# A longer estimate for sending rows out on GpSimd, and a mask of taken tokens read from PSUM

## The chip, the cores and the metric

One Trainium2 chip; the kernel runs on 1 of its cores. The metric is device microseconds of one execution, median of several runs. Engines: TensorE (PE, with PEld for its weight loads), VectorE (DVE), ScalarE (ACT), GpSimd (POOL) and SyncE (SP), each with its own instruction stream that runs in the written order; semaphores hold an instruction until what it needs is there.

## The reference

```python
def reference(**kwargs):
    attn_out = _attn_ref(**attn_kwargs)          # B 4, H 8, S 576, D 64
    x = np.ascontiguousarray(attn_out.transpose(0, 2, 1, 3)).reshape(B * S, H * D)
    x = _moe_ref(x=x, **moe_kwargs)              # g(x @ w_in) @ w_out, 2304 x 512, d_ff 2048
    return _moe2_ref(x=x, **moe2_kwargs)

def _moe2_ref(x, w_gate, w1, w2):
    N, D = x.shape                               # 2304, 512; E 8, F 1024
    cap = N // E                                 # 288
    logits = x @ w_gate
    order = np.argsort(-logits.flatten())
    assigned = -np.ones(N, dtype=np.int64)
    counts = np.zeros(E, dtype=np.int64)
    for idx in order:
        tok, e = (int(idx) // E, int(idx) % E)
        if assigned[tok] >= 0 or counts[e] >= cap:
            continue
        assigned[tok] = e
        counts[e] += 1
        if (assigned >= 0).all():
            break
    out = np.zeros((N, D), dtype=np.float32)
    for e in range(E):
        mask = assigned == e
        h = np.maximum(x[mask] @ w1[e], 0.0)
        out[mask] = h @ w2[e]
    return out.astype(np.float32)
```

Attention with a forgetting bias, a dense feed-forward layer, and a layer of eight experts in which every expert gets exactly 288 tokens, given out greedily by the largest logit.

## The kernel before

Class `Attention` (0 to about 325 us) and class `Ffn` (to about 725 us) compute the first two layers; the change leaves them alone. The last 340 us belong to class `Route`, which gives tokens to experts, and class `Experts`, which computes them.

**The router.** It works in eight phases; each fills one expert. A phase (`Route.phase`) searches the logit from which on the expert is full: five steps, each a compare of all tokens' best logits with up to 128 thresholds on VectorE (`cmp`, 128 x 18 x 128), 18 small matmuls on TensorE that count (`rp<-OH,cmp`, L1128), a readback on VectorE (`jk`), one more small matmul (`rp<-fl,ones`, L1156) and a few tiny VectorE instructions (`du`, `th`) that make the next thresholds. Then the tokens of the expert get their places (`s1`, zero for a token that isn't taken), a list of their rows is made (`row`, sent by SP as `idx`), the logits of the full expert are taken out, and the tokens that got a place are taken out of `alive`. Much of the router's state, `alive` among it, lies in one PSUM tile (`state`); `s1`, `nb`, `OH`, `cmp` and `wj` lie in SBUF. In before a token is dead if `nb = (s1 < cap + 0.5) * s1` is not zero: `nb` reads `s1` twice, and the next instruction multiplies `alive` with `nb == 0`.

**The experts.** For each expert the 288 rows are gathered on GpSimd's queue (`xg<-x2d,idx`, three indirect DMAs), transposed on TensorE (`pt`, L1422) and split into a high part on ScalarE (`xh`) and a low part on VectorE (`xl`). The weights come by SP in pieces of 128x512 (`raw`), eight buffers in all; ScalarE makes the high part `wh`, and while the router works GpSimd makes the low part `wl = raw - wh` (L1219 is the line of the helper that issues all of these; tiles tell them apart). First layer: 96 matmuls `ph` (L1441) of 288 columns, relu on ScalarE (`hh`), low part on VectorE (`hl`). Second layer: 96 matmuls `py` (L1493), copied out (`y`), turned back (`po`, `yo`), and sent out on GpSimd's queue in three indirect DMAs (`out_dram<-yo,idx`), each with a one-element memset of `spacer` ahead of it.

**What sets the order.** All instructions are written once, in Python, and each engine runs them in that order. `Experts` keeps a model clock for the core (`self.clock`) and one for each of VectorE, ScalarE and GpSimd (class `Queue`, L1187 on, which adds a duration for each issued instruction). `tick` moves the clock with each matmul; when the clock passes the time at which the router's next step should be ready, the step is written, and the low parts `hl`, `xl` and `wl`, gathers and weight loads are written when the model says that their inputs are there. `can_split` holds a weight piece back when GpSimd's model clock is 1500 ns ahead or a gather is due within 1300 ns. A changed duration in the model so moves instructions on all engines, without changing any of them.

Of the kernel before, what the change touches and what calls it, by code (L numbers as in the profile page):

```python
# [18 lines left out]
OP = mybir.AluOpType  # L19
AX = mybir.AxisListType  # L20
PSUM = bass.MemoryType.PSUM
DRAM = bass.MemoryType.DRAM
# [834 lines left out]
class Route:  # L857
# [22 lines left out]
    def t(self, shape, dt, name, bufs=1):  # L880
        if name not in self.STATE:
            return self.c.tile(shape, dt, name=name, bufs=bufs)
        n = math.prod(shape[1:]) * (2 if dt == BF16 else 4) // 4
        if name not in self.places:
            self.places[name] = [self.used + b * n for b in range(bufs)]
            self.used += bufs * n
            assert self.used <= 512
        at = self.places[name].pop(0)
        self.places[name].append(at)
        a = self.st[:, at:at + n]  # L890
        a = a if dt == F32 else a.bitcast(dt)
        return a if len(shape) == 2 else a.rearrange("p (a b) -> p a b", b=shape[2])
# [111 lines left out]
    def phase(self, k):  # L1004

        nc, J, E = self.nc, self.J, self.E
        v, t = self.v, self.t
        more = k < E - 1
        e1 = t([128, 1], F32, "e1")
        if more:  # L1010
            yield from self.search()

            n, pd = self.n, self.pd
            q = t([128, E], F32, "q8")
            v.scalar_tensor_tensor(q, pd[:, :E], n, self.rank, op0=OP.is_equal, op1=OP.mult)
            v.tensor_reduce(e1, q, axis=AX.X, op=OP.max)
        else:
            v.tensor_copy(e1, self.left)

        wj = t([128, J], F32, "wj")  # L1020
        v.tensor_scalar(wj, self.w2, e1, None, op0=OP.is_equal)
        AT = t([128, 2, J], F32, "AT")
        if more:
            v.scalar_tensor_tensor(AT[:, 0], self.mx, self.tau, wj, op0=OP.is_gt, op1=OP.mult)
            v.scalar_tensor_tensor(AT[:, 1], self.mx, self.tau, wj, op0=OP.is_equal, op1=OP.mult)
        else:
            v.tensor_copy(AT[:, 0], wj)
            v.tensor_scalar(AT[:, 1], wj, 0.0, None, op0=OP.mult)

        run = t([128, 2 * J], BF16, "run")  # L1030
        ATf = AT.rearrange("p a j -> p (a j)")
        v.tensor_tensor_scan(run, ATf, self.iotf[:, 0:2 * J], 0.0, op0=OP.add, op1=OP.bypass)
        self.mark()
        ei = t([128, 1], I32, "ei", bufs=8)
        v.tensor_scalar(ei, e1, -1.0, float(E), op0=OP.mult, op1=OP.add)

        self.out[k] = [ei, None, getattr(v, "t", 0)]
        yield 200


        pp = self.ps()
        nc.tensor.matmul(pp[:, 0:1], self.lower, run[:, J - 1:J], start=True, stop=True)
        nc.tensor.matmul(pp[:, 1:2], self.lower, run[:, 2 * J - 1:2 * J], start=True, stop=False)
        nc.tensor.matmul(pp[:, 1:2], self.higher, run[:, J - 1:J], start=False, stop=True)
        def close():

            if more:
                pe = t([128, E], F32, "pe")
                v.tensor_scalar(pe, self.rank, e1, -2 * self.BIG, op0=OP.is_equal, op1=OP.mult)
                v.tensor_tensor(self.L, self.L, self.bj(pe, E), op=OP.add)  # L1050
                yield from self.pause()
                yield from self.wishes()
                yield from self.pause()

        if k:
            yield from close()
        s1 = t([128, J], F32, "s1", bufs=2)
        sT = t([128, J], F32, "sT")
        v.scalar_tensor_tensor(s1, run[:, :J], pp[:, 0:1], AT[:, 0], op0=OP.add, op1=OP.mult)
        v.scalar_tensor_tensor(sT, run[:, J:], pp[:, 1:2], AT[:, 1], op0=OP.add, op1=OP.mult)  # L1060
        v.tensor_tensor(s1, s1, sT, op=OP.add)
        yield from self.pause()
        self.jobs += self.tokens(k, s1)
        if k in (0, 1, E - 2, E - 1):

            self.job()
            self.job()
            self.mark()
            yield 540
            self.job()  # L1070
            self.job()
        if not k:
            yield from close()
        if more:

            nb = t([128, J], F32, "nb")
            v.scalar_tensor_tensor(nb, s1, self.cap + 0.5, s1, op0=OP.is_lt, op1=OP.mult)
            v.scalar_tensor_tensor(self.alive, nb, 0.0, self.alive, op0=OP.is_equal, op1=OP.mult)
            v.tensor_tensor(self.OH, self.OH, self.bc(self.alive, E), op=OP.mult)
            if k < E - 2:  # L1080
                yield from self.pause()
                self.cmp = self.compare16(self.thr0)
            v.tensor_tensor(self.w2, self.w2, self.alive, op=OP.mult)
            v.tensor_tensor(self.left, self.left, e1, op=OP.subtract)
# [102 lines left out]
class Queue:  # L1187
# [9 lines left out]
    def __getattr__(self, name):  # L1197
        fn = getattr(self.eng, name)

        def issue(*a, **kw):  # L1200
            tiles = [x for x in (*a, *kw.values()) if hasattr(x, "tensor")]
            out, done = tiles[0], self.at.written
            n = max(math.prod(x.shape[1:]) for x in tiles)
            t = max(self.t, self.at.clock)
            for x in tiles[1:]:
                if x.space == PSUM and x.tensor.name != self.at.route.st.tensor.name:
                    t = max(t, self.at.clock + 190)
                elif (x.tensor.name, x.offset) in done:
                    eng, ns = done[x.tensor.name, x.offset]
                    t = max(t, ns + (130 if eng is self else 190))  # L1210
            fixed = self.fixed + (65 if any(math.prod(x.shape[1:]) == 1 for x in tiles[1:]) and n > 1 else 0)
            if name == "indirect_dma_start":
                self.t = t + self.fixed + 1000
            else:
                two = all(x.space != PSUM and (x.dtype in (I16, BF16) or name in ("tensor_scalar", "tensor_copy"))
                          for x in tiles)
                self.t = t + fixed + (self.fast if two else self.column) * n
            done[out.tensor.name, out.offset] = self, self.t
            return fn(*a, **kw)  # L1219

        return issue
# [438 lines left out]
```

## Time and profile before

| | |
|---|---|
| median of 3 runs | 1036.65 us (1034.18 to 1041.91) |
| profiled execution | 1032.85 us, span 1031.1 us |
| mean granted TensorE clock | 0.981 |
| TensorE busy | 964.3 us, 94% of the span |
| VectorE, ScalarE, GpSimd busy | 74%, 48%, 33% |

Times in rows are microseconds from the span's start, durations of single instructions in the tile view are nanoseconds. `[5.94 <-DVE cmp L1219]` behind a row means that the engine stood idle for 5.94 us before it, until that instruction was done. Rows of equal instructions that follow each other are merged (`x6`). The granted clock is a share of full speed; TensorE's two levels are 1.2 and 2.4 GHz. Matmuls overlap, so a row's duration is longer than the distance to the next row.

### The profile page before, as it was taken

The page shows a single profiled execution, that of the slowest core. Times are in us where ns is not written, and L with a number is a line of the kernel's source. Part 1 is how long each engine was busy: PE and PEld are TensorE (multiplying, and loading weights), DVE is VectorE, ACT ScalarE, POOL GpSimd, SP SyncE. Part 2 cuts the span into 40 slices and gives each one's busy share as a digit, 9 for nine tenths or more (in the row PEclk, how much of TensorE's full clock was granted, in tenths as well). Part 3 has the DMA queues.
Part 4 walks back from the last instruction along what each step waited for, and adds up shares of the span by engine and source line. Part 5 has one row for each costly group of instructions (what it writes and reads, how often), then busy time and mean ns, then how long its engine had stood idle before and what let it go on. Part 6 is the DMA issues. An engine that isn't in the chain of part 4 may idle for free.

```text
span 1031.1 us, 18509 instructions
## 1 busy us (share of the span) xinstructions
PE 964.3 (94%) x6479; PEld 854.7 (83%) x6479; DVE 768.1 (74%) x2109; ACT 490.2 (48%) x961; POOL 338.8 (33%) x391
## 2 busy tenths in 40 slices
PE   6899999999979999999999999999889978989995
PEld 5777777777767989899889898899789868979995
DVE  6688888878857669799999998875568777775410
ACT  5777777767745542332332323430345424546431
POOL 3144454534421000000000000330778858873211
PEclk9999999999989999999999999999999989999998
DMA  5768777776667140030121300102555436557300
GB/s 130 161 165 194 200 201 191 200 194 173 189 203 246 54 147 29 21 102 22 31 93 31 113 11 11 62 11 81 159 165 172 157 115 190 165 147 222 118 24 24
DMA packets 124347, 126.86 MB, mean 123 GB/s; under 512 B 74178, under 2 KB 90818, under 8 KB 124124
## 3 DMA queue, kind: packets, MB, share of 16 engines
q1 hardware_dynamic: 104604, 89.79, 30.7%
q0 software_dynamic: 18592, 34.75, 11.6%
q10 hardware_dynamic: 1056, 1.12, 0.4%
q8 instruction: 51, 0.84, 0.3%
q14 instruction: 44, 0.36, 0.1%
HBM read 93.55 MB, written 27.50 MB: 117 GB/s over the span
## 4 chain that ended last, share of the span: by engine, by line
PE 58%; DVE 24%; DMA 5%; issue 5%; ACT 5%; POOL 1%; SPq 1%; another core or an unknown queue 0%; POOLq 0%; ACTq 0%; DVEq 0%
PE py L1493 8%; PE ph L1441 8%; PE ph L620 8%; PE po L333 6%; PE pst L301 6%; DVE junk L682 6%; PE px L661 3%; PE px L663 3%; PE px L662 3%; ACT u L629 3%; PE ps L249 2%; PE ps L250 2%; DVE u L628 2%; DVE gl L642 2%; PE rp L1128 2%
## 5 line engine op out<-in xcount | busy, mean ns | idle before, releaser
L1219 POOL TENSOR_TENSOR wl<-raw,wh 128x512 fp32r<-128x512 f32 x98 | 129.2, 1345 | 57.7 <-DMA raw<-in_moe_w_dram 33.8
L629 ACT ACTIVATE u<-u,half 128x384 f32<-128x384 f32 x96 | 59.3, 617 | 173.8 <-DVE u L628 169.0
L620 PE MATMUL ph<-xh,ih 128*128 128x384 f32 x384 | 130.8, 341 | 3.6 <-ACT ih L584 3.6
L620 PE MATMUL ph<-xh,il 128*128 128x384 f32 x384 | 130.6, 340 | 0.2 <-DVE il L592 0.2
L620 PE MATMUL ph<-xl,ih 128*128 128x384 f32 x384 | 130.5, 340 | 0.0
L333 PE MATMUL po<-E,V 128*128 128x320 f32 (+4 forms) x448 | 113.9, 383 | 0.4 <-ACT E L305 0.4
L663 PE MATMUL px<-oh,gl 128*128 128x512 f32 x240 | 95.3, 397 | 3.7 <-DVE gl L642 3.7
L661 PE MATMUL px<-oh,gh 128*128 128x512 f32 x240 | 95.2, 397 | 1.9 <-ACT x L670 1.8
L662 PE MATMUL px<-ol,gh 128*128 128x512 f32 x240 | 94.5, 394 | 0.0
L333 PEld LDWEIGHTS po<-E,V 128*128 128x128 f32 (+1 forms) x448 | 75.9, 194 | 20.5 <-issue 7.8
L682 DVE SCALAR_TENSOR_TENSOR junk<-x,gb 128x512 f32<-128x512 f32 x120 | 84.9, 737 | 4.5 <-ACT x L670 4.5
L682 DVE SCALAR_TENSOR_TENSOR junk<-wt,gb 128x512 f32<-128x512 f32 x128 | 82.9, 685 | 0.0
L1493 PE MATMUL py<-hh,wh 128*128 128x288 f32 x256 | 81.0, 317 | 0.0
L1219 ACT ACTIVATE wh<-raw 128x512 fp32r<-128x512 f32 x128 | 75.9, 624 | 9.2 <-DMA raw<-in_moe_w_dram 8.0
L1441 PE MATMUL ph<-xh,wh 128*128 128x288 f32 x256 | 79.4, 310 | 0.4 <-ACT xh L1219 0.4
L1441 PE MATMUL ph<-xl,wh 128*128 128x288 f32 x256 | 79.0, 309 | 0.5 <-DVE xl L1219 0.4
L620 PEld LDWEIGHTS ph<-xh,ih 128*128 128x128 f32 x384 | 72.7, 189 | 8.0 <-ACT ih L584 3.9
L1441 PE MATMUL ph<-xh,wl 128*128 128x288 f32 x256 | 78.4, 306 | 0.0
L1493 PE MATMUL py<-hl,wh 128*128 128x288 f32 x256 | 77.5, 303 | 0.0
L1493 PE MATMUL py<-hh,wl 128*128 128x288 f32 x256 | 77.2, 302 | 0.0
L620 PEld LDWEIGHTS ph<-xl,ih 128*128 128x128 f32 x384 | 72.7, 189 | 3.4
L506 POOL TENSOR_TENSOR co<-cm,ce 128x512 f32<-128x512 f32 x32 | 40.5, 1264 | 104.2 <-ACT cm L505 99.4
(228 smaller groups left out, 2487.9 us busy)
## 6 DMA issues: line engine op xcount, KB each, us to landing
raw<-in_moe_w_dram SPq DMA_DIRECT2D x128, 256.0 KB
r<-in_moe_w_in_dram SPq DMA_DIRECT2D x16, 512.0 KB
r<-in_moe_w_out_dram SPq DMA_DIRECT2D x16, 512.0 KB
xg<-xd SPq DMA_DIRECT2D x6, 768.0 KB
x2d<-x SPq DMA_DIRECT2D x36, 128.0 KB
Y<-Y POOLq DMA_DIRECT2D x15, 288.0 KB
nk<-in_k_dram SPq DMA_DIRECT2D x32, 128.0 KB
nq<-in_q_dram SPq DMA_DIRECT2D x32, 128.0 KB
```

The costliest lines, as they stand in the source:

```text
L301: nc.tensor.matmul(pst[u][:, cols], l, r, start=first, stop=last, skip_group_check=u == "c" or u == "b")
L333: nc.tensor.matmul(t[:, 256 + c0:256 + g1], V[:b - a, kb, 64 * h:64 * h + 128], E[:b - a, e0:e0 + g1 - c0], start=i == 0, stop=i == len(or ...
L506: nc.gpsimd.tensor_tensor(out, f(m), f(e), op=OP.mult)
L620: nc.tensor.matmul(p[:, :G], a[:, s], b, start=n == 0, stop=n == 11)
L629: nc.scalar.activation(u, u, AF.Square, bias=self.half, scale=0.5)
L661: nc.tensor.matmul(px[t][:, cols], gh[:, s], oh[:, cols], start=i == 0, stop=False)
L662: nc.tensor.matmul(px[t][:, cols], gh[:, s], ol[:, cols], start=False, stop=False)
L663: nc.tensor.matmul(px[t][:, cols], gl[:, s], oh[:, cols], start=False, stop=last)
L682: self.nc.vector.scalar_tensor_tensor(junk, x(), 1.0, self.gb[:, e], op0=OP.mult, op1=OP.mult, accum_out=out[:, e:e + 1])
L1219: return fn(*a, **kw)
L1441: self.nc.tensor.matmul(p[:, :self.C], a[:, cols], b, start=c == 0 and i == 0, stop=c == 3 and i == 2)
L1493: nc.tensor.matmul(p[:, :C], a[:, o:o + 128], b[:, fb], start=fb == 0 and i == 0, stop=fb == 7 and i == 2)
```

## The change

Two edits. In the model of `Queue`, an indirect DMA whose target is in DRAM (a send-out) is charged 1300 ns instead of 1000; a gather keeps 1000. In `Route.phase`, the update of `alive` is written with three instructions in place of two: tokens not taken in this phase (`s1 < 0.5`) times `alive`, tokens beyond the capacity (`s1 > cap + 0.5`) times `alive`, and their sum. Every one of the three has one operand in PSUM.

```diff
@@ -1074,8 +1074,9 @@
         if more:
 
             nb = t([128, J], F32, "nb")
-            v.scalar_tensor_tensor(nb, s1, self.cap + 0.5, s1, op0=OP.is_lt, op1=OP.mult)
-            v.scalar_tensor_tensor(self.alive, nb, 0.0, self.alive, op0=OP.is_equal, op1=OP.mult)
+            v.scalar_tensor_tensor(nb, s1, 0.5, self.alive, op0=OP.is_lt, op1=OP.mult)
+            v.scalar_tensor_tensor(self.alive, s1, self.cap + 0.5, self.alive, op0=OP.is_gt, op1=OP.mult)
+            v.tensor_tensor(self.alive, nb, self.alive, op=OP.add)
             v.tensor_tensor(self.OH, self.OH, self.bc(self.alive, E), op=OP.mult)
             if k < E - 2:
                 yield from self.pause()
@@ -1210,7 +1211,7 @@
                     t = max(t, ns + (130 if eng is self else 190))
             fixed = self.fixed + (65 if any(math.prod(x.shape[1:]) == 1 for x in tiles[1:]) and n > 1 else 0)
             if name == "indirect_dma_start":
-                self.t = t + self.fixed + 1000
+                self.t = t + self.fixed + (1000 if tiles[0].space != DRAM else 1300)
             else:
                 two = all(x.space != PSUM and (x.dtype in (I16, BF16) or name in ("tensor_scalar", "tensor_copy"))
                           for x in tiles)
```

On VectorE, at the end of the first phase, the update of `alive` and what stands around it (`state` is the PSUM tile, `s_7787` is `s1`). Before:

```order
L1219 TENSOR_TENSOR OH<-state,w_7855 128x144
L1219 SCALAR_TENSOR_TENSOR nb<-s_7787 128x18
L1219 SCALAR_TENSOR_TENSOR state<-nb,state 128x18
L1219 TENSOR_TENSOR OH<-OH,state 128x144
L1219 TENSOR_TENSOR cmp<-mh,thr_4690 128x2304
```

And changed (all line numbers behind the edit are one higher):

```order
L1220 TENSOR_TENSOR OH<-state,w_7855 128x144
L1220 SCALAR_TENSOR_TENSOR nb<-s_7787,state 128x18
L1220 SCALAR_TENSOR_TENSOR state<-s_7787,state 128x18
L1220 TENSOR_TENSOR state<-nb,state 128x18
L1220 TENSOR_TENSOR OH<-OH,state 128x144
L1220 TENSOR_TENSOR cmp<-mh,thr_4690 128x2304
```

One instruction more stands ahead of `OH` and the first compare of the next phase, and none of the three reads two operands from SBUF.

On GpSimd, the end of the send-outs of expert 1 (the second ones of the program) and the low parts of expert 3 up to the gather of expert 3. Before:

```order
L1219 DMA out_dram<-yo,idx 2304x512
L1219 TENSOR_TENSOR wl_9556<-raw,wh_9555 128x512 x2
L1219 TENSOR_TENSOR wl_9622<-raw,wh_9621 128x512 x2
L1219 TENSOR_TENSOR wl_9677<-raw,wh_9676 128x512 x2
L1219 TENSOR_TENSOR wl_9736<-raw,wh_9735 128x512
L1219 DMA xg<-x2d_73,idx 96x512 x3
```

And changed:

```order
L1220 DMA out_dram<-yo,idx 2304x512
L1220 TENSOR_TENSOR wl_9483<-raw,wh_9482 128x512
L1220 TENSOR_TENSOR wl_9586<-raw,wh_9585 128x512 x2
L1220 TENSOR_TENSOR wl_9653<-raw,wh_9652 128x512 x2
L1220 TENSOR_TENSOR wl_9686<-raw,wh_9685 128x512 x2
L1220 TENSOR_TENSOR wl_9765<-raw,wh_9764 128x512 x2
L1220 DMA xg<-x2d_73,idx 96x512 x3
```

One low part of expert 2 has moved behind the send-outs and one of expert 3 ahead of the gather: nine low parts stand there instead of seven.

On TensorE, the second phase of the router beside the first rows of expert 0 (`busy` fills time, `pt` transposes gathered rows, `ones` is the second small matmul of a search step). Before, from its count on, which is written directly ahead of the first row below:

```order
L1422 MATMUL pt<-identf,xg 128x96 x6
L1441 MATMUL ph<-xh_8045,wh_7848 128x288
L1156 LDWEIGHTS ones
L1156 MATMUL rp<-fl,ones 128x1
L1441 MATMUL ph<-xl_8046,wh_7848 128x288
```

And changed, where the count (18 pairs of a weight load and a matmul, of which the first pair is shown) comes after them:

```order
L1413 MATMUL busy<-wh_7955 128x288 x4
L1423 MATMUL pt<-identf,xg 128x96 x6
L1442 MATMUL ph<-xh_8023,wh_7848 128x288
L1129 LDWEIGHTS cmp
L1129 MATMUL rp<-OH,cmp 128x8
```

The transposes and the first expert matmul, which wait for gathered rows, have moved ahead of the count.

## Rows read from the trace of the kernel before

**Rows 1.** Windows of the last stages: us, then busy us (count) per engine, PEclk, DMA.

```profile
720.00:820.00 100.00, 91.62 (x874) 84.43 (x873) 67.09 (x220) 44.09 (x94) 78.46 (x70) 0.97 0.52 158
820.00:840.00 20.00, 14.06 (x147) 13.13 (x146) 16.80 (x37) 6.10 (x13) 12.07 (x11) 0.83 0.55 175
840.00:940.00 100.00, 92.05 (x888) 86.64 (x887) 70.28 (x224) 49.50 (x107) 74.96 (x67) 0.98 0.56 167
940.00:1020.00 80.00, 79.81 (x613) 79.50 (x612) 26.66 (x53) 32.24 (x75) 13.24 (x21) 1.00 0.25 83
```

**Rows 2.** Waits of TensorE, 733 to 1020 us: total us, times, longest.

```profile
PE rp L1128 <- DVE cmp L1219: 8.4, 5, 5.9
...
PE rp L1147 <- DVE f L1219: 2.6, 1, 2.6
PE pt L1422 <- DMA xg<-x2d,idx: 2.0, 3, 1.0
```

**Rows 3.** Tile `nb`: duration ns min/median/max, first and last start.

```profile
L1219 DVE SCALAR_TENSOR_TENSOR nb<-s x7: 167/1030/1280, 721.6 to 921.0; 128x18 f32<-128x18 f32 x7
L1219 DVE SCALAR_TENSOR_TENSOR state<-nb,state x7: 181/181/182, 721.8 to 922.1; 128x18 f32<-128x18 f32 x7
```

**Rows 4.** Tile `cmp`, the second compare of each search.

```profile
L1219 DVE TENSOR_TENSOR cmp<-mh,th x7: 1357/1761/7445, 696.7 to 890.8; 128x2304 bf16<-128x2304 bf16 x7
```

**Rows 5.** Timeline of VectorE: start us, us.

```profile
733.40 0.15 DVE L1219 TENSOR_SCALAR du<-rp 128x1 int32<-128x1 f32 x1
...
756.61 1.19 DVE L1219 SCALAR_TENSOR_TENSOR nb<-s 128x18 f32<-128x18 f32 x1
...
787.84 1.23 DVE L1219 SCALAR_TENSOR_TENSOR nb<-s 128x18 f32<-128x18 f32 x1
...
823.87 7.45 DVE L1219 TENSOR_TENSOR cmp<-mh,th 128x2304 bf16<-128x2304 bf16 x1
...
921.02 1.03 DVE L1219 SCALAR_TENSOR_TENSOR nb<-s 128x18 f32<-128x18 f32 x1
```

**Rows 6.** Timeline of GpSimd: a gather, send-outs and two chains of low parts.

```profile
763.78 0.91 POOL L1219 DMA_INDIRECT xg<-x2d,idx  x1 [6.01 <-PE py L1493]
...
781.10 0.94 POOL L1219 DMA_INDIRECT out_dram<-yo,idx  x1 [0.17 <-issue]
...
782.35 0.93 POOL L1219 DMA_INDIRECT out_dram<-yo,idx  x1 [0.21 <-issue]
...
786.48 12.24 POOL L1219 TENSOR_TENSOR wl<-raw,wh 128x512 fp32r<-128x512 f32 x8 [0.63 <-ACT wh L1219]
...
822.68 7.42 POOL L1219 TENSOR_TENSOR wl<-raw,wh 128x512 fp32r<-128x512 f32 x6
```

**Rows 7.** Timeline of TensorE: idle times before router matmuls, and matmuls at both speeds.

```profile
728.25 0.59 PE L1128 MATMUL rp<-OH,cmp 128*128 128x8 bf16 x18
...
731.88 0.55 PE L1422 MATMUL pt<-identf,xg 96*128 96x96 f32 x4 [0.77 <-DMA xg<-x2d,idx]
...
759.68 0.61 PE L1128 MATMUL rp<-OH,cmp 128*128 128x8 bf16 x18 [0.34 <-DVE cmp L1219]
...
791.55 0.61 PE L1128 MATMUL rp<-OH,cmp 128*128 128x8 bf16 x18 [0.81 <-DVE cmp L1219]
...
831.37 0.65 PE L1128 MATMUL rp<-OH,cmp 128*128 128x8 bf16 x18 [5.94 <-DVE cmp L1219]
...
832.26 0.44 PE L1441 MATMUL ph<-xl,wh 128*128 128x288 f32 x1
...
835.05 0.44 PE L1441 MATMUL ph<-xh,wh 128*128 128x288 f32 x1
...
835.53 0.30 PE L1441 MATMUL ph<-xh,wl 128*128 128x288 f32 x1
...
887.78 0.61 PE L1128 MATMUL rp<-OH,cmp 128*128 128x8 bf16 x18 [0.77 <-DVE cmp L1219]
...
924.11 0.16 PE L1042 MATMUL rp<-run,lower 128*128 128x1 bf16 x1 [0.60 <-DVE ei L1219]
```

## The prediction

> **What bounds the kernel now.** I read the windows of the last stages first, then the waits of TensorE there, the tiles of the instructions that the change edits, and last the timelines of VectorE, GpSimd and TensorE around the waits. The windows [rows 1]: from 940 us on TensorE is full (79.81 of 80 us, 613 matmuls, 0.13 us each), while from 720 to 940 us, where the router still works and experts 0 to 4 are computed, it stands idle for 8.4, 5.9 and 8.0 us in the three pieces. Only those 22 us can be won. TensorE runs its matmuls in one written order, so when a router matmul comes before VectorE has its operand ready, everything behind it stands too. The list of waits says so: 8.4 us of idle time ended with a compare on VectorE, five times, one of them 5.9 us; 2.6 us ended with a result of the last search step, 2.0 us with gathered rows [rows 2].
>
> **Why VectorE is late.** The instruction that marks tokens as taken, `nb`, reads `s1` twice, both from SBUF. Its seven runs take 167 ns at least, 1030 ns at the median and 1280 ns at most, while its successor on the same 128x18, which reads one operand from the router's state in PSUM, takes 181 or 182 ns every time [rows 3]. The long ones lie beside GpSimd's low parts `wl`: `nb` at 787.84 ends at 789.07, inside a chain of eight low parts that ran without a pause from 786.48 on [rows 5, 6]. So an instruction with two SBUF inputs waits for GpSimd. The compares do too: `cmp<-mh,th` takes 1.36 us at least, 1.76 at the median and once 7.45 us [rows 4]. That one began at 823.87, 1.2 us into a burst of six low parts (7.42 us, 1.24 each), and ended at 831.32, 1.2 us after the burst's end at 830.10: it was passed over at each of the five boundaries between low parts [rows 5, 6].
>
> The Trainium skill ("SBUF — State Buffer", section "Who interferes with whom") says that two SBUF inputs contend with a GpSimd instruction that reads SBUF, and that the later one is blocked until the first has finished. The rows of `nb` agree (1.28 us is one low part), the row of 7.45 us does not: by the rule that compare would have waited for one low part, some 1.3 us, and by the rule no such long wait can come in the new order either. By the row it can, and my chances below go by the row.
>
> **The change, part by part.** The estimate: the planner charges a send-out 60+1000 ns and 62 for the memset ahead of it, 1.12 us, from now on 1.42; two of them start 1.25 us apart [rows 6], so the old figure is short by 0.13 us and the new one long by 0.17. It adds no instruction. It moves the planner's clock of GpSimd by 0.9 us after each expert's three send-outs, and with it where the next low parts, gathers and, through them, ScalarE's and TensorE's instructions are written. The other edit: `nb` takes `alive` from PSUM as its second tensor, a second instruction does the same, and a third adds the two; seven times two instructions become three.
>
> The terms, in the time of the profiled execution (span 1031.1 us, 1032.85 with what lies around it, 3.8 us under the median 1036.65):
>
> - The long compare. TensorE stood 5.94 us for it [rows 7]. The granted clock of that window is 0.83 [rows 1], a mean of its two levels (1.2 and 2.4 GHz), and the expert matmuls read 0.44 us instead of 0.30 from 832.26 to 835.05 [rows 7]: 3.4 us at half speed after the idle stretch, 1.7 lost. Both orders put a burst and this compare near each other, but in the new one the second send-outs are followed by nine low parts before the gather, not seven, and some twenty more expert matmuls (20 x 0.13 = 2.6 us) stand ahead of the phase's first count, so the compare meets the burst elsewhere. I take the wait as gone: 7.6 us. Bounds: 0 (it stays) to 7.6.
> - `nb`. Four of the seven were long, from 756.61 (1.19 us) to 921.02 (1.03) [rows 5]. With 0.18 for the new form and 0.20 for the added instruction each of these phases gets 0.65 to 0.9 us earlier. TensorE gets of it at most the idle time that it has right behind: 0.34, 0.81, 0.77 and 0.60 us [rows 7], sum 2.5. In the other three phases the added instruction costs 0.2 us each, of which I let two thirds reach TensorE: 0.4. Net 2.1. An addition onto `alive` does not stand in the trace of before: its nearest row is 0.18 (one operand in PSUM, never late in seven runs [rows 3]); if it waited for a low part as `nb` did, 1.28, seven times without cover, 9 us would be lost. I take 0.2, the nearest row. Bounds: 2.5 to -9.
> - The new written order. In phase 1 it puts the router's counting matmuls behind six transposes of gathered rows and a first expert matmul. Today that count is done at 728.84; TensorE then waits for the gather up to 731.88, and the next router value `du` is there at 733.40 [rows 5, 7]. Behind the transposes the count runs from about 732.8 (0.6 us), and with the readback (0.3) and four expert matmuls at half speed (0.24 apart) ahead of the next small one `du` comes at 734.4 to 734.5, 1.0 us later. I charge 1.0, though expert matmuls may cover it. Bounds: 0 to 14, the idle time of rows 1 that the terms above leave (22.3 - 5.9 - 2.5 = 13.9), taken once more.
> - Gathers. Expert 1's gather stands one low part (1.25 us) later on GpSimd, but GpSimd was idle for 6.01 us ahead of it [rows 6], so it does not come later. Its first transposes are written six matmuls later, so 0 to 0.8 us of the 2.0 us waited [rows 2] come back; I take 0, since the rows land as before. The index list of expert 3 goes out behind one more weight load on SP's queue, and its gather behind two more low parts (2.5 us), which cover that.
>
> Sum: 7.6 + 2.1 - 1.0 = 8.7 us, which makes 1024.2 in the profiled execution and 1028.0 against the median. What is late next is small: the same matmuls waiting some tenths for each step of the search.
>
> **Rivals.**
> A. The passing over comes back at another place. For it: of seven later compares at least four waited (median 1.76), and one of them was passed over [rows 4]; nothing in the new order keeps them clear, and the burst behind the second send-outs gets longer. Against it: the others got in at the next boundary. A wait like the old one costs 7.6 us: 1028.0 + 7.6 = 1035.6. The same number comes out if compare and burst keep their places, because both follow TensorE's order, and only `nb` and the written order count.
> B. Slower than before: the compare meets the nine low parts behind the second send-outs in their first one and is passed over to their end. That is three more than the six of before, 3.7 us, on top of the wait as it was: 1035.6 + 3.7 = 1039.3. It is slower than before from the first low part beyond the old six on (1036.8). Against it: ScalarE must have all nine high parts ready, and in before the seventh was not.
> C. Expert 1's rows are no longer waited for, since the later GpSimd clock writes all their transposes later: 2.0 us [rows 2], and with no idle stretch no fall of the clock behind it, 1.5 more. 1028.0 - 3.5 = 1024.5. Against it: the rows themselves land no earlier.
>
> **Chances.** The forecast 0.48, its own range 1021 to 1033; A 0.28; B 0.10; C 0.14. A measurement of this kernel tells about 1% (10.4 us) from no change, so faster means under 1026.3: four tenths of the forecast (0.19) and nearly all of C (0.13), 0.32. Slower means over 1047.0: two long waits in one run, within A and B, 0.06. The rest, 0.62. The range: down to 1019, C with 5 us of the small waits gone as well; up to 1041, B with 2 us of small waits more.
>
> **What would show it.** Right: `nb` at 170 to 190 ns in all seven phases, no compare over 2.7 us (1.36 and one low part), no TensorE wait over 3 us from 733 us on, a granted clock near 1.00 where it was 0.83, idle time of TensorE between 720 and 940 us near 14 us instead of 22. Wrong: a compare of 4 us or more; or, without one, waits of TensorE for counts that sum to more than 8.4 us, and then the written order sets the time and not the shared port. An `nb` that still reaches 1 us would fell the second term.

## The result, and the profile after

The changed kernel takes 1025.34 us, median of 6 runs (1021.07 to 1030.34); the kernel before, measured beside it, 1038.56 (1034.18 to 1042.4). The ratio is 0.987, 95% interval 0.984 to 0.990. Two later comparisons of the same two kernels gave 0.997 (0.994 to 1.000) and 0.988 (0.984 to 0.993). The forecast was 1028.0 us, its own range 1021 to 1033.

The profiled execution took 1030.13 us, one of the two longest of the six and 4.8 us above their median; that of the kernel before, 1032.85, is 5.7 us below the median of the runs beside it. So the two traces laid side by side here are 2.7 us apart, not 13.2, and no trace shows the changed kernel at the speed of its median. The windows of the last stages, to be laid beside [rows 1]:

```profile
720.00:820.00 100.00, 91.60 (x858) 84.82 (x857) 63.20 (x210) 43.61 (x93) 75.97 (x67) 0.93 0.49 148
820.00:840.00 20.00, 20.00 (x215) 18.92 (x214) 15.27 (x54) 8.83 (x19) 17.15 (x16) 1.00 0.75 227
840.00:940.00 100.00, 91.98 (x848) 87.58 (x847) 75.67 (x225) 49.82 (x107) 71.95 (x69) 0.93 0.57 169
940.00:1020.00 80.00, 77.63 (x596) 77.07 (x595) 24.38 (x49) 30.97 (x72) 11.94 (x20) 1.00 0.23 75
```

The stretch from 820 to 840 us is full now, at a granted clock of 1.00 where it was 0.83. But the two pieces around it are as idle as before, and their granted clock fell to 0.93 (0.97 and 0.98 before). Idle time from 720 to 940 us: 8.4 + 0 + 8.0 = 16.4 us, where 22.3 stood before and 14 was forecast. The waits of TensorE from 733 to 1020 us, beside [rows 2], say what they ended with:

```profile
PE rp L1042 <- DVE ei L1220: 7.7, 3, 3.7
PE py L1494 <- DVE hl L1220: 1.8, 1, 1.8
PE pt L1423 <- DMA xg<-x2d,idx: 1.7, 2, 1.0
PE rp L1129 <- DVE cmp L1220: 0.9, 1, 0.9
```

The waits for compares shrank from 8.4 to 0.9 us. In their place TensorE waits 7.7 us for `ei`, the end of a short VectorE chain at the beginning of each phase. The 3.3 us for `jk`, the readback on VectorE, which stood second in the list of the kernel before and which I had left out of [rows 2], are gone too:

```profile
PE rp L1156 <- DVE jk L1219: 3.3, 4, 1.3
```

The tiles of VectorE, beside [rows 3, 4]:

```profile
L1220 DVE SCALAR_TENSOR_TENSOR nb<-s,state x7: 152/165/174, 720.5 to 921.4; 128x18 f32<-128x18 f32 x7
L1220 DVE TENSOR_TENSOR state<-nb,state x7: 181/181/182, 720.8 to 921.7; 128x18 f32<-128x18 f32 x7
...
L1220 DVE TENSOR_TENSOR cmp<-mh,thr x7: 1347/1351/1991, 691.8 to 889.0; 128x2304 bf16<-128x2304 bf16 x7
L1220 DVE TENSOR_TENSOR cmp<-mh,th x7: 1357/1360/2315, 695.6 to 894.4; 128x2304 bf16<-128x2304 bf16 x7
...
L1220 DVE TENSOR_SCALAR wj<-w,e x8: 238/459/4249, 712.9 to 922.7; 128x18 f32<-128x18 f32 x8
```

`nb` is short in all seven phases, the added instruction costs 0.18 us, and no compare of `mh` takes over 2.32 us. The long instruction is now `wj`, which marks the tokens that wish for this phase's expert and reads `w2` from SBUF. VectorE's two long ones:

```profile
844.63 4.25 DVE L1220 TENSOR_SCALAR wj<-w,e 128x18 f32<-128x18 f32 x1
...
877.34 3.99 DVE L1220 TENSOR_SCALAR wj<-w,e 128x18 f32<-128x18 f32 x1
```

GpSimd beside them:

```profile
840.47 0.92 POOL L1220 DMA_INDIRECT xg<-x2d,idx  x1 [0.30 <-issue]
841.41 7.43 POOL L1220 TENSOR_TENSOR wl<-raw,wh 128x512 fp32r<-128x512 f32 x6
...
872.89 0.92 POOL L1220 DMA_INDIRECT xg<-x2d,idx  x1 [0.30 <-issue]
873.83 7.46 POOL L1220 TENSOR_TENSOR wl<-raw,wh 128x512 fp32r<-128x512 f32 x6
```

And TensorE behind them:

```profile
849.76 0.16 PE L1042 MATMUL rp<-run,lower 128*128 128x1 bf16 x1 [3.68 <-DVE ei L1220]
851.21 0.44 PE L1494 MATMUL py<-hh,wh 128*128 128x288 f32 x1
...
882.21 0.16 PE L1042 MATMUL rp<-run,lower 128*128 128x1 bf16 x1 [3.47 <-DVE ei L1220]
882.67 0.44 PE L1494 MATMUL py<-hh,wh 128*128 128x288 f32 x1
```

Each `wj` began in the third of six low parts and ended, like the compare of 7.45 us in the kernel before, only when the whole chain was over (848.88 against 841.41 + 7.43 = 848.84; 881.33 against 881.29): it was passed over by three further low parts. Each time TensorE stood still, and its expert matmuls then ran at 0.44 us instead of 0.30, the lower clock. So in this execution the passing over went from one place to another, and its two waits sum to 7.15 us.

### The profile page after: what moved, and what is told of

Its sections match the earlier page's. It is cut to its first block, busy times and chain, and to the rows that moved or that the text cites. A ratio compares the mean times of both kernels' runs of the same rounds, so it can differ in the third digit from the quotient of the medians.

```text
span 1028.4 us, 18522 instructions
## 1 busy us (share of the span) xinstructions
PE 967.3 (94%) x6480; PEld 858.3 (83%) x6480; DVE 766.2 (75%) x2117; ACT 490.6 (48%) x961; POOL 337.7 (33%) x390
## 3 DMA queue, kind: packets, MB, share of 16 engines
q10 hardware_dynamic: 1056, 1.12, 0.4%
## 4 chain that ended last, share of the span: by engine, by line
PE 57%; DVE 21%; DMA 7%; issue 6%; ACT 5%; POOL 3%; SPq 1%; POOLq 0%; ACTq 0%; DVEq 0%
PE py L1494 9%; PE ph L1442 8%; PE ph L620 8%; PE po L333 6%; DVE junk L682 6%; PE pst L301 6%; PE px L661 3%; PE px L663 3%; PE px L662 3%; ACT u L629 3%; PE ps L249 2%; DVE u L628 2%; DVE gl L642 2%; PE ps L250 2%; DVE u L640 2%
## 5 line engine op out<-in xcount | busy, mean ns | idle before, releaser
L1494 PE MATMUL py<-hh,wl 128*128 128x288 f32 x256 | 79.5, 311 | 0.0
```

What stands on the lines that cost most here:

```text
L1494: nc.tensor.matmul(p[:, :C], a[:, o:o + 128], b[:, fb], start=fb == 0 and i == 0, stop=fb == 7 and i == 2)
```

## The experiments

The theory: what can be won between 720 and 940 us is VectorE being held by GpSimd's low parts, and the change takes some of it away. Rivals: the new written order is the gain; or the gain is a difference between two sets of runs.

### 1 to 4: each edit alone

`e1_old_order_new_nb` takes the three new instructions into the kernel before without moving anything else (`quiet` charges the planner for the two old ones without issuing them):

```diff
+            v.quiet = True
             v.scalar_tensor_tensor(nb, s1, self.cap + 0.5, s1, op0=OP.is_lt, op1=OP.mult)
             v.scalar_tensor_tensor(self.alive, nb, 0.0, self.alive, op0=OP.is_equal, op1=OP.mult)
+            v.quiet = False
+            nc.vector.scalar_tensor_tensor(nb, s1, 0.5, self.alive, op0=OP.is_lt, op1=OP.mult)
+            nc.vector.scalar_tensor_tensor(self.alive, s1, self.cap + 0.5, self.alive, op0=OP.is_gt, op1=OP.mult)
+            nc.vector.tensor_tensor(self.alive, nb, self.alive, op=OP.add)
```

> Every engine's written order is that of before; only the update of alive is issued in its new form (three instructions with one operand in PSUM), while the planner is still charged for the old two. Port theory (what the change gains is time that VectorE instructions with two SBUF inputs lose to GpSimd's low parts): no nb over 0.2 us, TensorE's idle time behind the four long nb gone (2.5 us less 0.4), so 2 us under before, ratio 0.996 to 0.999, and more only if the compare that was passed over for 7.45 us is missed by chance. Order theory (the new written order gains it): 1.000, at most 1 us off. In both the compare after the second send-outs can still be passed over.

`e2_new_order_old_nb` is the reverse: the changed kernel's order, charged for the three instructions, with the two old ones issued.

> Every engine's written order is that of the changed kernel; only the update of alive is issued in its old form (two instructions, the first with two SBUF inputs). Port theory: nb is long again in about four of seven phases (1.0 to 1.3 us), 2 to 4 us over the changed kernel, ratio to before 0.989 to 0.992. Order theory: the ratio of the changed kernel, 0.987, within 0.001.

`e3_nb_alone` is the changed kernel with the old estimate, `e4_estimate_alone` the kernel before with the new one; in both the planner makes an order of its own.

```diff
-                self.t = t + self.fixed + (1000 if tiles[0].space != DRAM else 1300)
+                self.t = t + self.fixed + 1000
```

> The new update of alive with the planner's old charge of 1000 ns for send-outs, so another written order. If the update carries the gain: ratio 0.985 to 0.990. If the longer estimate carries it: 0.996 to 1.000. A wait of 4 us or more of a wj or a compare beside low parts would add 4 to 5 us to a run either way.

> The longer estimate of 1300 ns with the old update of alive. If the estimate carries the gain: ratio 0.985 to 0.990. If the update carries it: 0.997 to 1.002, with nb still at a median of about 1 us.

Measured, 12 runs each against 35 runs of the kernel before (1031.84 us):

| | median us | ratio | 95% interval |
|---|---|---|---|
| new `nb` in the old order | 1029.66 | 0.998 | 0.996 to 1.000 |
| old `nb` in the new order | 1031.60 | 0.999 | 0.996 to 1.002 |
| new `nb`, old estimate | 1029.68 | 0.999 | 0.996 to 1.002 |
| old `nb`, new estimate | 1029.95 | 0.998 | 0.996 to 1.001 |

None of them is shown to differ from the kernel before, and none has the 0.987; the changed kernel itself was not run in this set. For the second neither theory's ratio came (0.987, or 0.989 to 0.992), and its old `nb` was long less often than expected, as was that of the fourth (medians 0.21 and 0.25 us, against 1.03 in the trace of the kernel before). The first fits the term of `nb` (2.1 us; 0.998 of 1031.84 is 1.9 us less, interval -0.4 to 4.1), but doesn't prove it: the fourth, with the old `nb`, has the same ratio. What the tiles of the first show is that `nb` does what it should, and that no compare of `mh` was passed over, although the written order is the old one:

```profile
L1081 DVE SCALAR_TENSOR_TENSOR nb<-s,state x7: 152/174/175, 719.3 to 916.8; 128x18 f32<-128x18 f32 x7
L1083 DVE TENSOR_TENSOR state<-nb,state x7: 181/182/182, 719.6 to 917.1; 128x18 f32<-128x18 f32 x7
...
L1227 DVE TENSOR_TENSOR cmp<-mh,thr x7: 1348/1354/1674, 690.6 to 882.9; 128x2304 bf16<-128x2304 bf16 x7
L1227 DVE TENSOR_TENSOR cmp<-mh,th x7: 1357/1486/1935, 694.4 to 887.6; 128x2304 bf16<-128x2304 bf16 x7
```

Its `wj` was passed over instead, in the old order too:

```profile
809.05 4.42 DVE L1227 TENSOR_SCALAR wj<-w,e 128x18 f32<-128x18 f32 x1
```

The same stands in the profiled runs of the second (4.44 us) and the fourth (4.42); the third had none (its longest compare of `mh` took 2.86 us), and its profiled run, at 1024.0 us, was the fastest of its twelve. So the long wait is not tied to an order: it was seen in both, and the compare of 7.45 us is in one of the two traces of the old order. That left open whether the 0.987 was of the kernel or of its set of runs.

### 5 and 6: the changed kernel again, and `wj` with an operand in PSUM

> The changed kernel as it is, in the same run as the next kernel. Theory whole (the two edits together give the 1.3 per cent that each alone did not): a ratio of 0.984 to 0.990 again, as in the first comparison. Rival session (part of the 0.987 belonged to that comparison: its runs of the kernel before stood at 1038.6 us, those of the next comparison at 1031.8): the ratio comes out at 0.992 to 0.998, near the kernels with one edit. In a profiled run: nb at 165 ns in all seven places under either; if any DVE operation is passed over by low parts, it is wj, for 4 us.

`e6_wj_psum` changes nothing but the form of `wj` (the planner is charged for the old form, so the order of every engine is that of the changed kernel):

```diff
+        v.quiet = True
         v.tensor_scalar(wj, self.w2, e1, None, op0=OP.is_equal)
+        v.quiet = False
+        nc.vector.scalar_tensor_tensor(wj, self.w2, e1, self.alive, op0=OP.is_equal, op1=OP.mult)
```

> The changed kernel with one more instruction form: wj with alive (PSUM) as its third operand, written order untouched. Theory passing-over (wj waits for GpSimd's low parts, sometimes for a whole chain of them): all eight wj at 0.2 to 0.3 us, no TensorE wait over 3 us from 733 us on the router's transposes, TensorE idle 720 to 1018 us of 12 to 14 us where the profiled run of the change had 17.0, the highest runs missing, and 3 to 6 us less than the changed kernel run beside it (about 0.995 of its median). Rival shift (the compares take over the waiting, as wj took it over here): wj short, but a cmp or another two-input operation of 4 us or more and the median within 2 us of the changed kernel. Rival nothing (passing-over happens in one run in several only): median within 2 us, the highest runs alone lower.

The changed kernel: 1031.36 us against 1032.10, ratio 0.997 (0.994 to 1.000), 12 runs against 23, as the rival "session" has it; its profiled run had one `wj` of 4.44 us. With the new `wj`: 1033.72 us, 1.000 (0.997 to 1.003), so the 3 to 6 us that I expected were not won. Its `wj` does what it should:

```profile
L1024 DVE SCALAR_TENSOR_TENSOR wj<-w,e,state x8: 233/234/235, 710.7 to 925.1; 128x18 f32<-128x18 f32 x8
```

but now a compare was passed over in the profiled run, the first of a search:

```profile
852.52 4.95 DVE L1226 TENSOR_TENSOR cmp<-mh,thr 128x2304 bf16<-128x2304 bf16 x1
```

It ended at 857.47, after the last of nine low parts (856.25) by 1.2 us, about its own time:

```profile
845.05 11.20 POOL L1226 TENSOR_TENSOR wl<-raw,wh 128x512 fp32r<-128x512 f32 x9
856.20 0.09 POOL L1226 MEMSET spacer<- 1x1 f32 x1
```

That fits the rival "shift": with one instruction taken off, another one was passed over, as far as this one profiled run shows.

### 7 and 8: the wait by itself

Two kernels that compute nothing of the reference: GpSimd runs chains of low parts, and one VectorE instruction of the form of `wj`, of `nb` or of the compare begins at a chosen time beside them.

> A kernel of its own that computes nothing of the reference: five low parts (128x512, two SBUF operands) on GpSimd, and one DVE operation that begins at four different times while the first of them runs; the high parts of the other four lie ready long before, or come from ScalarE about 0, 0.4 or 0.8 us later. Theory chain (a DVE operation gets in only when GpSimd has nothing ready at that moment): with all high parts ready the tensor_scalar of wj's form takes 4 to 6 us in most places, with the second high part late at most 1.3 us. Theory first operation (it waits for the low part that runs, no longer): at most 1.3 us in all places, whatever is ready. scalar_tensor_tensor of nb's form: at most 1.3 us under either as far as the traces so far show. Compare of cmp<-mh's form: 1.35 us when alone, at most 2.6 us by first operation, over 4 us in some places by chain. With one PSUM operand: 0.2 to 0.3 us everywhere.

> Again a kernel of its own that computes nothing of the reference: chains of six low parts on GpSimd, and one DVE operation that begins 0 to 3.5 us after the chain, in steps of some 80 ns, so that it meets the first, the second and the third low part at every point, the handover from one to the next among them; with all high parts ready, with high parts that ScalarE makes one per us, and with memsets in place of all low parts but the first. Every second trial loads four 128x512 blocks beside it. Theory handover (a request that arrives while GpSimd passes from one low part to the next is passed over to the end of the chain, as the 7.45 us compare of the kernel before, which began 0.07 us before a low part): over 4 us in the trials within some 0.1 us of a handover, at most 1.3 us of waiting in all others. Theory queue (passed over when the next low part had its operands before the request and another followed without a gap, as all six wj of 4.0 to 4.4 us): over 2.5 us in most trials that meet the second or a later low part with high parts ready. Theory none of it (something else of the kernel is needed): at most 1.3 us of waiting in every trial. Memsets: no waiting under any theory, if a memset does not hold what the DVE operation waits for.

In the first no instruction waited over 1.2 us, whether the next high parts were ready or late, so the theory "chain" falls, and the form with a PSUM operand took 0.22 us in all eight trials. The second has 258 trials with low parts, which meet the first four of a chain of six (the tensor_scalar the start of the fifth as well) in steps of some 80 ns, with holes of up to 0.3 us, and 0.5 us at the tensor_scalar's start. The three forms (`ts` like `wj`, `stt` like `nb`), up to the last of these trials:

```profile
L72 DVE TENSOR_SCALAR ts<-a,e x86: 235/756/1359, 9.5 to 1828.3; 128x18 f32<-128x18 f32 x86
L74 DVE SCALAR_TENSOR_TENSOR stt<-a,b x86: 167/744/1286, 479.7 to 2192.7; 128x18 f32<-128x18 f32 x86
L76 DVE TENSOR_TENSOR cmp<-mh,th x86: 1348/1934/2470, 950.7 to 2604.6; 128x2304 bf16<-128x2304 bf16 x86
```

The longest of each is its shortest and 1.12 us, less than one low part (1.25): 1359 - 235, 1286 - 167, 2470 - 1348. Nothing was passed over, at none of the handovers met, and neither with high parts ready nor with late ones. So two more theories of mine fall, that of the handover and that of the queue; by these trials something else in the kernel is needed. One trial did show the passing over, which no theory expected of it, with memsets in place of all low parts but the first:

```profile
2609.47 1.26 POOL L101 TENSOR_TENSOR wl<-raw,wh 128x512 fp32r<-128x512 f32 x1 [1.10 <-ACT pa L89]
...
2609.95 3.14 DVE L72 TENSOR_SCALAR ts<-a,e 128x18 f32<-128x18 f32 x1
2610.67 2.38 POOL L99 MEMSET wl<- 128x512 f32 x5
```

The tensor_scalar waited through the low part and all five memsets. In the six trials after it, which began later and later in the same chain, it took 0.51 to 1.42 us instead of 0.24, so memsets held it there too, though less long. The form of `nb` in the same place did not (1.27 us), and where the first low part was over, memsets held neither that form (0.17 us) nor the compare (1.35 us).

### 9 and 10: both orders with nothing to wait for

So memsets can stand in for the low parts, if `wj` has its PSUM form. `e9_zero_low_after` is the changed kernel, `e10_zero_low_before` the one before, both with these two edits; the planner is charged as before them, and no other instruction of any engine moves. The low parts of the weights made on GpSimd are zero here.

```diff
-        eng.tensor_tensor(lo[:, cols], raw, f(hi)[:, cols], op=OP.subtract)
+        if eng is self.g:
+            eng.quiet = True
+            eng.tensor_tensor(lo[:, cols], raw, f(hi)[:, cols], op=OP.subtract)
+            eng.quiet = False
+            self.nc.gpsimd.memset(f(lo)[:, cols], 0.0)
+        else:
+            eng.tensor_tensor(lo[:, cols], raw, f(hi)[:, cols], op=OP.subtract)
```

> The changed kernel with every GpSimd low part (raw less its high part, from SBUF) replaced by a memset of the same block to zero, so that the experts' low parts are left out, and with wj in its form with a PSUM operand; every engine's written order else as in the changed kernel. No vector operation then stands beside a GpSimd operation that reads SBUF. Theory waiting on GpSimd (what is left in the two kernels between 720 and 1020 us is DVE operations held by low parts): compares of cmp<-mh at 1.35 us, no TensorE wait over 3 us from 733 us, TensorE idle 720 to 1018 us of 10 to 13 us, and 6 to 11 us less than the changed kernel beside it (some 1020 us against 1031). Rival order (the idle time is the order's own, transfers and evictions): within 3 us of the changed kernel.

> The same two edits in the kernel before, whose written order stays: with no DVE operation held, what is left between this kernel and the last one is the written order and one more short instruction per expert. Theory order is worth little (1 us, as the prediction took it): within 2 us of the last kernel, and 8 to 13 us below the kernel before. Rival order is the gain: 4 us or more above the last kernel.

Measured, 6 runs each, with the changed kernel itself as a fourth beside them (`e12_after_third`, below):

| | median us | ratio to before | 95% interval |
|---|---|---|---|
| before (11 runs) | 1035.99 | | |
| changed | 1025.25 | 0.988 | 0.984 to 0.993 |
| before, zero low parts | 1013.85 | 0.980 | 0.975 to 0.984 |
| changed, zero low parts | 1014.08 | 0.979 | 0.975 to 0.983 |

Two things follow. Without low parts the two written orders come out 0.2 us apart; the spread of their runs leaves some 4 us either way, so the rival "order", which asked for 4 us or more, is not borne out. And against its own version with zero low parts the kernel before loses 1035.99 - 1013.85 = 22.1 us, where I had expected 8 to 13, and the changed one 1025.25 - 1014.08 = 11.2. Each of these two differences is uncertain by some 4.5 us, by the spread of the runs. In this set, then, the gain of 10.7 us is of the size of the smaller loss beside GpSimd's low parts. In the changed kernel without them TensorE was full from 820 to 940 us, at full clock:

```profile
820.00:840.00 20.00, 20.00 (x217) 19.12 (x215) 15.83 (x53) 9.19 (x20) 9.57 (x17) 1.00 0.77 250
840.00:940.00 100.00, 100.00 (x957) 95.71 (x956) 75.08 (x245) 57.77 (x126) 39.53 (x69) 1.00 0.61 194
```

and every compare took its shortest time:

```profile
L1226 DVE TENSOR_TENSOR cmp<-mh,thr x7: 1348/1350/1353, 690.9 to 879.4; 128x2304 bf16<-128x2304 bf16 x7
L1226 DVE TENSOR_TENSOR cmp<-mh,th x7: 1357/1357/1360, 694.7 to 883.9; 128x2304 bf16<-128x2304 bf16 x7
```

In the kernel before without them the idle time of 720 to 820 us alone was left, 8.7 us:

```profile
720.00:820.00 100.00, 91.30 (x847) 84.01 (x847) 60.62 (x210) 43.68 (x94) 38.80 (x69) 0.91 0.47 149
820.00:840.00 20.00, 20.00 (x225) 18.54 (x224) 14.42 (x51) 8.60 (x19) 13.20 (x25) 1.00 0.64 216
840.00:940.00 100.00, 100.00 (x950) 96.43 (x949) 73.63 (x234) 58.00 (x127) 34.96 (x61) 1.00 0.64 199
```

One reservation: the memsets are also shorter than the low parts (0.54 us against 1.29 at the median), and they read neither `raw` nor `wh`, for which GpSimd waited 33.8 and 23.5 us in the kernel before. So gathers and send-outs stand less long behind them. No wait of TensorE from 733 us on was put down to GpSimd in either kernel, and the wait for gathered rows did not shrink (1.7 us in the changed kernel, 3.2 with zero low parts; 2.0 and 3.9 in the other order), so I take that share as small; it was not measured apart.

### 11 and 12: a spacer, and the changed kernel a third time

`e11_spacer` puts a one-element memset behind every low part:

```diff
         eng.tensor_tensor(lo[:, cols], raw, f(hi)[:, cols], op=OP.subtract)
+        if eng is self.g and hasattr(self, "spacer"):
+            self.nc.gpsimd.memset(self.spacer, 0.0)
```

> The changed kernel with a one-element memset on GpSimd behind every low part of the expert stage, some 0.09 us each; no other engine's order moves. Theory handover (a DVE operation is passed over where one low part follows the other without a gap): no DVE operation held over 1.3 us, 3 to 6 us less than the changed kernel beside it. Theory other (memsets keep a tensor_scalar out as well, as a chain of five memsets did for 2.97 us in the kernel of its own): waits of 4 us on wj or a compare stay, median within 2 us of the changed kernel or above it by the memsets' own time.

> The changed kernel once more, beside the three above and against the kernel before. Theory part session: a ratio of 0.993 to 0.999, as in its second comparison. Rival whole: 0.984 to 0.990, as in its first.

1025.77 us with spacers, 1025.25 without: nothing is won. `wj` was passed over as before:

```profile
845.17 4.75 DVE L1220 TENSOR_SCALAR wj<-w,e 128x18 f32<-128x18 f32 x1
```

with a memset between any two of the low parts, two of which stand here:

```profile
844.84 1.29 POOL L1220 TENSOR_TENSOR wl<-raw,wh 128x512 fp32r<-128x512 f32 x1
846.07 0.09 POOL L1341 MEMSET spacer<- 1x1 f32 x1
846.12 1.26 POOL L1220 TENSOR_TENSOR wl<-raw,wh 128x512 fp32r<-128x512 f32 x1
```

The changed kernel itself gave 0.988 here, as the rival "whole" has it. So 0.987, 0.997 and 0.988 stand side by side, from three sets of runs, the last two of them on different chips. The kernel before took 1038.6, 1032.1 and 1036.0 us in them, the changed one 1025.3, 1031.4 and 1025.3. Why the second set has hardly a gain is open. The loss beside the low parts depends on which instruction meets which low part, and one such wait is 4 us of TensorE's time, a third of the gain; but only one run of each set has a profile, so that it was this is not shown. The three profiled runs of the changed kernel differ in another place as well, the first wait for gathered rows: from the first `nb` to the first `du` behind it TensorE stood idle for 2.9, 5.1 and 2.8 us. The second set's run is the one with 5.1, so the place where the new order puts a count behind gathered rows is a candidate too.

## Why the prediction was right, and where it was not

**What bounds the kernel**: right, and by more than I claimed. I read the 22 us of idle time as VectorE being late, mostly through low parts; without low parts the kernel before is 22.1 us faster. That the two numbers agree is chance. Of the idle time 8.7 us remain without low parts, the granted clock from 720 to 820 us was lower then (0.91 against 0.97), and 3.7 of the 19.2 us between the two profiled runs lie ahead of the first compare (692.9 and 689.2 us), where the two kernels differ in nothing but GpSimd's first memsets.

**The long compare, 7.6 us**: gone as a compare (at most 2.32 us), and 820 to 840 us run at a clock of 1.00, as the signs asked. But the step "I take the wait as gone" failed in all three profiled runs of the changed kernel, and with it the sign "no TensorE wait over 3 us": the passing over came back as two `wj`, 7.15 us of idle time in the first and 7.4 (3.89 + 3.49) in the third set's, and as one `wj` of 4.44 us in the second's. That is rival A, at a place I had not named. I had looked for it among the compares because `wj` took 0.24 us in the kernel before and 1.08 at most, and had not asked which other instructions can be held. Nor is my reason shown, that the new order moves the compare away from the burst: the old order with the new `nb` had no long compare either (1.94 us at most).

**`nb`, 2.1 us**: 152 to 174 ns in seven of seven, and the addition 181, as taken; the bound of -9 us did not come up. Alone it measured 1.9 us, but with an interval that takes in zero, so its worth is not shown.

**The new written order, -1.0**: the delay came as reckoned where I looked for it. Behind the first `nb` the first `du` comes 11.83 us later in the kernel before and 12.94 in the changed one:

```profile
721.57 0.17 DVE L1219 SCALAR_TENSOR_TENSOR nb<-s 128x18 f32<-128x18 f32 x1
...
720.47 0.17 DVE L1220 SCALAR_TENSOR_TENSOR nb<-s,state 128x18 f32<-128x18 f32 x1
...
733.41 0.16 DVE L1220 TENSOR_SCALAR du<-rp 128x1 int32<-128x1 f32 x1 [0.89 <-PE rp L1157]
```

By the clock of the trace `du` is as early as before (733.40 [rows 5]), but only because this run was 1.1 us ahead at `nb`. The old order with the new `nb` has 11.83 us again; the changed kernel's other two traces have 16.89 and 13.37:

```profile
718.44 0.16 DVE L1220 SCALAR_TENSOR_TENSOR nb<-s,state 128x18 f32<-128x18 f32 x1
...
735.33 0.16 DVE L1220 TENSOR_SCALAR du<-rp 128x1 int32<-128x1 f32 x1 [1.20 <-PE rp L1157]
```

What of it reaches the total is open. TensorE's idle time there is the same in the first and third of these traces as in the kernel before (2.9 and 2.8 us against 2.9), and the two orders without low parts are 0.2 us apart, give or take 4.

**Gathers, 0**: right; 1.7 us of waiting against 2.0.

**Rivals.** B did not come up: no compare met the nine low parts from their first on. C did not either, the rows were still waited for. A came up, in every profiled run of the changed kernel. Its 1035.6 is against the median; in the time of the profiled execution, in which my terms are written, it is 1024.2 + 7.6 = 1031.8 us, and the three took 1030.1, 1035.1 and 1031.5. So the traces look like rival A, and the medians of the first and third set, 1025.3, lie below it.

**The sum, 8.7 us**: measured were 13.2, 0.7 and 10.7 between the medians of the three sets. The forecast lies among them, and the spread is wider than any single term. That 1025.34 fell into the range of 1021 to 1033 is so in part luck: the wait that makes up most of the sum, and that I took as gone, came back in every profiled run, the faster runs have no profile, and the second set's 1031.36 lies in the range with hardly a gain behind it. The 0.62 for a change within 1% fits one set of three; the other two are faster by 1.2 and 1.3%, for which I had given 0.32.

**The rule weighed.** By the Trainium skill ("SBUF — State Buffer", section "Who interferes with whom") the later instruction is blocked until the first has finished. The kernel of its own agrees in all its 258 trials with low parts (1.12 us at most). The rows of this case that do not agree are the compare of 7.45 us, `wj` of 3.99 to 4.75 us, the compare of 4.95 and the tensor_scalar of 3.14 beside memsets. To let the chances go by the row was right: long waits did come in the new order.

## What to carry to other kernels

Before you take a wait on a shared resource as gone, list every instruction that could be held in its place, and measure the whole price of the resource once, with the disturbing instruction replaced by one that does not disturb: here 22 us before and 11 after, while each edit alone, in another set of runs, showed next to nothing. A change whose worth depends on which instruction meets which other one should be measured in more than one set of runs. An instruction moved to a PSUM operand (`nb`, `wj`) was never held, so moving operands does work instruction by instruction. With `wj` moved as well nothing more was won here, since a compare was held next; that it would pay once the last such instruction has moved was not tried.

## What the runs showed of the hardware that I had not expected

In the traces of this kernel a held VectorE instruction got in at the end of the low part that ran, or only at the end of the whole chain. In the ten traces with low parts I count 76 `nb`, `wj` and `cmp<-mh` from 700 us on that began while a low part ran and took 0.3 us or more above the shortest of their form. Of these 65 got in at the next boundary or the one after it, 11 were passed over to the end; behind 13 of the 65 no further low part followed, so they could not have been. Ten of the 11 began 1.2 to 3.5 us after GpSimd had issued its last indirect DMA (as `wj` at 844.63, 3.24 us after the gather that ended at 841.39), the eleventh 8.7 us after; of the 65 others only 7 began within 4 us of one. In the kernels of their own, which had no indirect DMA, no instruction was passed over by low parts. That speaks for the transfer that follows such an issue as the missing condition; it was not tried. Against it stands the eleventh, and the tensor_scalar that five memsets kept out with no indirect DMA in the kernel. And nine of the 11 are `wj`, each behind a gather, five of them in the same phase, so the DMA and what else comes at that place of the written order are not told apart.

The holding goes both ways: beside a compare a low part took up to 2.48 us instead of 1.25 in the second kernel of its own. And a memset on GpSimd does not hold the forms of `nb` and of the compare, but it does hold the tensor_scalar of `wj`'s form, and five in a row kept one out for 2.4 us.
